# Seventeen loads of a recurrence-and-feed-forward kernel, issued by ScalarE in place of SyncE

## The chip, the core and the metric

One core of one Trainium2 chip. A core has five engines that run beside each other and meet through semaphores: TensorE (PE, matmuls), VectorE (DVE), ScalarE (ACT), GpSimd (POOL) and SyncE (SP, which here only issues transfers). Sixteen DMA engines move the data. A transfer is issued by an instruction of SP or of ACT, each of which has a queue of its own to the DMA engines. The metric is the device time of one execution in microseconds, median of the runs; less is better.

## The reference, cut to what matters

```python
# 4 batches, 8 heads, 768 positions, 48 channels
for t in range(S):
    state = alpha[:, :, t, :, None] * state + np.einsum('bhd,bhe->bhde', k[:, :, t], v[:, :, t])
    y[:, :, t] = np.einsum('bhd,bhde->bhe', q[:, :, t], state)
x = y.transpose(0, 2, 1, 3).reshape(3072, 384)
h = np.maximum(np.maximum(x @ w1, x @ w2), x @ w3)      # 384 -> 768
out = h @ w_out                                         # 768 -> 384
```

A gated linear recurrence over 768 positions, then a feed-forward layer that takes the maximum of three products. All tensors are float32.

## The kernel before, in words

The positions are cut into 6 blocks of 128. A *unit* is one block of one batch, with its 8 heads: 24 units, u = 0 to 23. Two neighbouring units make a *group*, n = 0 to 11, and are loaded together.

For each group four tensors are loaded: a (alpha), k, q and v, 128 positions by 16 heads by 48 channels, 384 KB each. A row of one head has 48 floats, so every piece that the DMA engines move has 192 bytes. Groups 0 to 3 are loaded in halves of 192 KB (one unit each; "load k 2 8" is the second half of k of group 2), groups 4 to 11 whole. There are four buffers of each tensor, so the load of group n waits until group n - 4 has been read. The weights (four matrices of 1.2 MB, in two pieces each) are loaded among the first two groups.

What is done with a unit, with the lines of the profile:

- ACT takes the logarithm of a (L398, "ln"); PE sums it along the positions (L438, "cums" and L408, "totals"); ACT takes exponentials (L443 "ep", L446 "en", L414 "e").
- DVE or POOL multiply q and k by them (L450); POOL or ACT scales v (L457, L460).
- PE turns the scaled q and k (L479), or a DMA transpose does ("cross", L469, issued by SP); ACT or DVE copies them (L486).
- PE makes the scores (L495), DVE masks them (L500), PE multiplies with v and adds what the state gives (L541, L538, "outs"); the state itself is carried by L600, L607 and L613.
- The result is copied (L552, L554), turned (L568, L573) and goes through the feed-forward layer: PE (L638, "grow"), ACT (L649) and DVE (L654), then PE (L674, "shrink"), a copy by ACT or DVE (L689) and the store (L694), 192 KB a unit.

The feed-forward layer uses w2 - w1 and w3 - w1, and w1 @ w_out folded into one matrix (L329, L337, L362, L368, L379, L386).

Every step is entered in a `Plan` with a list of engines that could do it. The table `ORDER` gives the order in which the steps are put into the program, and `PICK` the place in that list of the engine taken, where it is not the first. Each engine then runs its own instructions in that order and waits by semaphores. So a step's place in `ORDER` sets only its place among the instructions of its own engine. `load_options` lists who can issue a load: before, SP alone. Stores can be issued by ACT or SP. The transfers of SP and ACT share eight semaphores in turn, by their order in `ORDER`: a transfer waits until the one that stands eight before it has landed, whichever engine issued that.

SP issues its transfers strictly one after the other: an issue that waits holds back those behind it. The same holds for ACT, where an issue stands between computing steps.

Of the kernel before, what the change touches and what calls it, by code (L numbers as in the profile page):

```python
# [32 lines left out]


ORDER = (
# [44 lines left out]
)  # L80
BANKS = (
# [9 lines left out]
)  # L91
PICK = {
# [8 lines left out]
}  # L101

HARD, HARD_LOAD, HARD_LATE, LATE_FROM = 0.5, 1.8, 1.5, 3


def load_options(share, n):
    return [("SP", HARD, 0, HARD_LOAD * share, HARD_LATE * (n >= LATE_FROM))]  # L110


def weight_options(share, cast):
# [57 lines left out]
def kernel(  # L171
# [125 lines left out]
    def load(n):  # L297
        cb, g = divmod(n, B // UB)
        pieces = [(i * H, (i + 1) * H) for i in range(UB)] if n < HALF_LOADS else [(0, HG)]
        for lo, hi in pieces:  # L300
            for x in "akqv":
                t = ld[x][n % LOADED]
                plan.step(f"load {x} {n} {lo}", load_options((hi - lo) / HG, n), n,
                          lambda e, x=x, t=t, lo=lo, hi=hi: engines[e].dma_start(  # L304
                              t[:, lo:hi],
                              views[x][cb * P:(cb + 1) * P, g * HG + lo:g * HG + hi]),
                          writes=[(x, n % LOADED, h) for h in range(lo // H, hi // H)])
# [455 lines left out]
```

## Time and profile before

| | |
|---|---|
| time, median of 3 runs | 152.29 us (152.26 to 152.42) |
| span of the profiled execution | 466.5 us (its time beside the span is not given) |
| TensorE busy in it | 457.5 us, 1683 matmuls |
| VectorE, ScalarE, GpSimd busy | 112.5, 90.1, 48.0 us |
| loads and weights (queue of SP) | 27.27 MB in 113232 packets |
| stores and constants of ACT (queue of ACT) | 3.54 MB in 2880 packets |
| packets under 512 bytes | 109712 of 116131 |

The span runs from the first to the last instruction. In this profiled execution it is three times as long as a timed run. A row of the timeline gives start, length, engine, line, operation and tile; SPq and ACTq are the issues of transfers by SP and ACT, and the length of such a row is the time that the issuing engine spends on it, not the transfer. "Us to landing" is the time from the issue to the last byte.

### The profile page before, as it was taken

To read this page: it belongs to the slowest core of one execution; us is meant where nothing else is said; L and a number is where in the kernel's file an instruction comes from. 1 tells how busy PE (TensorE), PEld (TensorE's weight loads), DVE (VectorE), ACT (ScalarE), POOL (GpSimd) and SP (SyncE) were. 2 spreads that over 40 slices of the span, in tenths; PEclk is the share of its full clock that TensorE was granted. 3 is DMA by queue.
4 is the path that set the end of the run, shared out by engine and by line. 5 is a ranking of instruction groups with operands and counts; after the bars stand their busy time and mean duration, and the time that the engine had idled before them with its cause. 6 is when DMAs were issued, how large, how long until landed. Compare 5 with 4: busy or idle time off the path is not lost.

```text
span 466.5 us, 4171 instructions
## 1 busy us (share of the span) xinstructions
PE 457.5 (98%) x1683; PEld 263.5 (56%) x1683; DVE 112.5 (24%) x196; ACT 90.1 (19%) x177; POOL 48.0 (10%) x72
## 2 busy tenths in 40 slices
PE   4999999999999999999999999999999999999997
PEld 1667556674555656547546645545546554567473
DVE  5420313131123122222412221322221321231100
ACT  4323221122121312111212200121220111001010
POOL 0110002003001030210111120011110020000000
DMA  9999500540087000700032640020550030100001
GB/s 179 272 287 209 110 0 1 111 76 1 0 163 124 1 0 18 152 17 35 0 60 49 141 91 9 2 62 0 112 112 17 18 79 25 35 0 25 1 34 34
DMA packets 116131, 31.07 MB, mean 67 GB/s; under 512 B 109712, under 2 KB 114960, under 8 KB 116112
## 3 DMA queue, kind: packets, MB, share of 16 engines
q1 hardware_dynamic: 113232, 27.27, 27.9%
q10 hardware_dynamic: 2880, 3.54, 2.2%
q8 instruction: 13, 0.21, 0.2%
q14 instruction: 6, 0.05, 0.0%
HBM read 23.69 MB, written 4.72 MB: 61 GB/s over the span
## 4 chain that ended last, share of the span: by engine, by line
PE 98%; DMA 1%; SPq 0%; DVE 0%; issue 0%; DVEq 0%
PE psum L638 38%; PE psum L674 29%; PE psum L479 6%; PE psum L495 4%; PE psum L582 4%; PE psum L541 3%; PE psum L438 3%; PE psum L568 3%; PE psum L600 3%; PE psum L538 2%; PE psum L379 2%; DMA qn<-in_q_dram 1%; PE psum L362 1%; PE psum L408 1%; SPq L304 0%; DVE qk L450 0%
## 5 line engine op out<-in xcount | busy, mean ns | idle before, releaser
L638 PE MATMUL psum<-xT,wd 128*128 128x256 f16 (+1 forms) x540 | 186.4, 602 | 0.0
L638 PEld LDWEIGHTS <-wd 128*128 128x128 f16 x540 | 105.1, 209 | 67.5 <-issue 61.5
L674 PE MATMUL psum<-wo,hT 128*128 128x384 f16 (+1 forms) x150 | 96.7, 887 | 0.0
L674 PEld LDWEIGHTS <-hT 128*128 128x128 f16 x150 | 34.4, 230 | 54.6 <-issue 52.0
L674 PE MATMUL psum<-w1o,xT 128*128 128x384 f16 (+1 forms) x75 | 50.1, 847 | 0.0
L654 DVE TENSOR_TENSOR hT<-psum,hT 128x512 f16<-128x512 f32 (+1 forms) x39 | 24.7, 647 | 99.7 <-PE psum L638 99.7
L649 ACT ACTIVATE hT<-psum 128x512 f16<-128x512 f32 (+1 forms) x39 | 21.7, 564 | 111.0 <-PE psum L638 111.0
L500 DVE TENSOR_TENSOR LA<-psum,c 128x1024 f16<-128x1024 f32 x24 | 28.9, 1221 | 41.0 <-PE psum L495 28.7
L541 PE MATMUL psum<-v,LA 128*128 128x48 f16 x192 | 30.3, 314 | 0.0
L541 PEld LDWEIGHTS <-LA 128*128 128x128 f16 x192 | 26.5, 179 | 5.7 <-issue 5.1
L613 POOL TENSOR_TENSOR Z<-U,G 48x192 f16<-48x192 f32 x26 | 14.1, 543 | 109.5 <-DVE U L607 108.5
L438 PE MATMUL psum<-la,c 128*128 128x384 f16 x24 | 19.9, 847 | 4.3 <-ACT la L398 4.3
L479 PE MATMUL psum<-c,qk 128*128 128x128 f16 x96 | 22.1, 480 | 1.7 <-DVE qk L450 1.7
L479 PEld LDWEIGHTS <-qk 128*128 128x128 f16 x96 | 16.9, 208 | 9.1 <-DVE qk L450 4.0
L450 POOL TENSOR_TENSOR qk<-qn,ep 128x384 f16<-128x384 f32 x11 | 10.9, 994 | 105.2 <-ACT ep L443 94.0
L674 PEld LDWEIGHTS <-xT 128*128 128x128 f16 x75 | 13.1, 185 | 14.7 <-issue 14.2
L582 PE MATMUL psum<-Z 128*128 128x384 f16 x27 | 20.2, 869 | 0.0
L443 ACT ACTIVATE ep<-psum 128x384 f32<-128x384 f32 x24 | 11.7, 494 | 41.3 <-PE psum L438 41.2
L689 ACT COPY ob<-psum 128x384 f32<-128x384 f32 (+1 forms) x18 | 8.3, 469 | 54.7 <-PE psum L674 54.7
L554 DVE TENSOR_SCALAR xb<-psum,c 128x384 f16<-128x384 f32 x15 | 9.2, 617 | 37.9 <-PE psum L541 37.9
L568 PE MATMUL psum<-c,xb 128*128 128x128 f16 x63 | 17.5, 455 | 0.0
L446 ACT ACTIVATE en<-psum 128x384 f32<-128x384 f32 x24 | 11.5, 490 | 28.4 <-PE psum L438 27.1
(61 smaller groups left out, 297.2 us busy)
## 6 DMA issues: line engine op xcount, KB each, us to landing
out_dram<-ob ACTq DMA_DIRECT2D x17, 192.0 KB, 1.9
an<-in_alpha_dram SPq DMA_DIRECT2D x8, 384.0 KB, 5.3
kn<-in_k_dram SPq DMA_DIRECT2D x8, 384.0 KB, 5.4
qn<-in_q_dram SPq DMA_DIRECT2D x8, 384.0 KB, 5.7
vn<-in_v_dram SPq DMA_DIRECT2D x8, 384.0 KB, 4.2
ws<-in_moe_w_dram SPq DMA_DIRECT2D x3, 768.0 KB, 6.7
an<-in_alpha_dram SPq DMA_DIRECT2D x8, 192.0 KB, 4.0
kn<-in_k_dram SPq DMA_DIRECT2D x8, 192.0 KB, 4.0
```

What stands on the lines that cost most here:

```text
L438: nc.tensor.matmul(live[Lk], tri, la[:, hs, :D], start=True, stop=True)
L479: nc.tensor.transpose(live[tk][:, w, j, :], qk[:, w, 2 * j:2 * j + 2, :], ident)
L495: nc.tensor.matmul(live[Ak][:, p, j * P:(j + 1) * P], qkT[rows, 1, j, :], qkT[rows, 0, j, :], start=True, stop=True)
L500: lambda e: nc.vector.tensor_mul(LA.rearrange("p a b t -> p (a b) t"), live[Ak].rearrange("p a (b t) -> p (a b) t", t=P), maskA.unsqueeze( ...
L541: nc.tensor.matmul(yp[:, 2 * j + p, :], LA[:, p, j, :], v16[:, 2 * j + p, :], start=(cb == 0), stop=True, skip_group_check=True)
L568: nc.tensor.transpose(live[xk][:, ft, :], xb[:, ft * P:(ft + 1) * P], ident)
L582: nc.tensor.matmul(live["wm"], zero[:, :P], zero, start=True, stop=True)
L613: lambda e, rows=rows, cols=cols: engines[e].tensor_mul(Zn[rows, :, cols], (Us[u % 3] if cb else live[pk])[rows, :, cols], G[rows, i * NP: ...
L638: nc.tensor.matmul(live[gk][:, jj, :], wd[:, kt, g, j * P:(j + 1) * P], xT[:, kt, :], start=(kt == 0), stop=(kt == NFT - 1))
L649: lambda e, h=h, gk=gk: nc.scalar.activation(out=h, in_=live[gk], func=AFT.Relu),
L654: lambda e, h=h, gk=gk: nc.vector.tensor_max(h, live[gk], h),
L674: nc.tensor.matmul(live[ok][:, cols], a[:, i * P:(i + 1) * P], w[:, cols], start=(kt == 0), stop=(kt == nk - 1))
```

## The change

`load_options` gets ACT as a second choice, and `PICK` takes it for seventeen loads: six halves (of groups 2 and 3) and eleven whole ones (of groups 4 to 11). All of them stand behind the loads of the weights. About half of them stand where a packet of TensorE's instructions comes. `ORDER` places them, and some stores, anew among the steps of ACT.

```diff
 def load_options(share, n):
-    return [("SP", HARD, 0, HARD_LOAD * share, HARD_LATE * (n >= LATE_FROM))]
+    return [("SP", HARD, 0, HARD_LOAD * share, HARD_LATE * (n >= LATE_FROM)), ("ACT", 0.45, 0, HARD_LOAD * share)]
 PICK = {
...
+    19: 1, 21: 1, 25: 1, 27: 1, 28: 1, 30: 1, 235: 1, 300: 1, 365: 1, 367: 1,
+    486: 1, 488: 1, 544: 1, 545: 1, 547: 1, 604: 1, 662: 1,
...
 }
```

What this makes of the engines' programs: PE, DVE and POOL have the same instructions in the same order. ACT has its computing steps in the same order, with the seventeen loads between them; ten or so of its stores stand some steps earlier or later. SP has seventeen issues fewer. By their order the moved loads are: k 2 (second half), a 3 (second half), v 2 (first half), k 3 (first half), q 3 (second half), v 3 (first half), and then q 4, k 5, k 6, v 6, v 8, a 9, k 8, k 9, k 10, v 9 and k 11. A part of the order on ACT, where the first of them stand:

```diff
 L649 Activation hT
+L304 DMACopy kn<-in_k_dram 128x8x48
 L414 Activation e
 L398 Activation la<-an 128x8x48
...
 L446 Activation en
+L304 DMACopy an<-in_alpha_dram 128x8x48
 L414 Activation e
+L304 DMACopy vn<-in_v_dram 128x8x48
 L649 Activation hT
```

105 rows, old and new, of tables (ORDER, PICK) are left out of this document.

## The prediction

> **What bounds the kernel now.** I read the engine totals and the granted clock first, because the span and the times do not fit.
>
> ```profile
> span 466.5 us, 4171 instructions
> PE 457.5 (98%) x1683; PEld 263.5 (56%) x1683; DVE 112.5 (24%) x196; ACT 90.1 (19%) x177; POOL 48.0 (10%) x72
> core 0: 466.5 us, clock 1.000
> 68.74 0.63 PE psum L438
> ```
>
> The span is 466.5 us and the median of the runs is 152.29 us. The page gives no other time for the profiled execution. The clock column reads 1.000, yet TensorE (PE) is busy 457.5 us, which cannot fit into 152.29, so PE ran at least three times slower there than in the timed runs. The profile's shares are therefore not those of the timed run: a stage that PE bounds shrinks, what the DMA engines and the other engines need does not. So I work out differences and add them to the median.
>
> The second view is the DMA row and the stages by window.
>
> ```profile
> DMA  9999500540087000700032640020550030100001
> 0.00:34.00 34.00, 28.00 (x132) 16.31 (x133) 14.85 (x35) 12.23 (x20) 3.98 (x8) 1.00 0.99 247
> 34.00:53.00 19.00, 19.00 (x86) 13.53 (x82) 1.76 (x2) 5.79 (x10) 1.00 (x1) 1.00 1.04 206
> 160.00:350.00 190.00, 190.00 (x683) 105.61 (x682) 47.62 (x76) 37.35 (x74) 26.54 (x38) 1.00 0.25 53
> ```
>
> The columns are the length, then the busy time of PE, PEld, DVE, ACT and POOL, the clock, the DMA share and GB/s. Up to 53 us the 16 DMA engines are full (0.99 and 1.04). That stretch does not shrink with a faster PE: it is a floor under the start.
>
> How much faster PE is follows from the first load of group 2, a 2, and its reader.
>
> ```profile
> 27.49 3.81 SPq L304 DMA_DIRECT2D an<-in_alpha_dram  x2
> an<-in_alpha_dram SPq DMA_DIRECT2D x1, 192.0 KB, 6.5
> 68.42 0.95 PE L438 MATMUL psum<-la,c 128*128 128x384 f16 x1
> L398 ACT ACTIVATE la<-an 128x384 f16<-128x384 f32 x8 | 4.1, 524 | 2.2 <-DMA an<-in_alpha_dram 2.2
> ```
>
> a 2 lands at 27.49 + 6.5 = 34.0; its logarithm takes 0.52, so the matmul "cums 4" (at 68.42 in the profile) cannot start before 34.5 in a timed run. Behind it stand 466.5 - 68.4 = 398.1 us of the profile. They fit into 152.29 - 34.5 = 117.8 us, so r, the length of PE's work in a timed run over that in the profile, is at most 117.8 / 398.1 = 0.296. I take 0.25 to 0.296. The lower end is an estimate: at 0.25 the 398.1 take 99.5, and 18.3 us are left for PE's waits, the last stores and what lies outside the span, more than I can account for.
>
> The Trainium skill, "TensorE: Matmul & The Clock Gate", section "Seeing it yourself", reports the clock gate stuck at a quarter for 50 us and more. 384 columns in 0.63 us are 610 a microsecond, a quarter of that page's 2.4 GHz, so the trace agrees although the clock column shows nothing; by it r would be 0.25, an estimate.
>
> So a timed run has two parts: a start of about 34.5 us that the DMA engines set, and a rest of PE's order with waits. In 160 to 350, PE would need 190 x 0.25 to 0.296 = 47.5 to 56.2 us, DVE is busy 47.6 and ACT 37.4. DVE is near its limit and ACT has a fifth to a third free.
>
> **The change part by part.** By the order of the programs, PE, DVE and POOL are untouched, and ACT's computing steps keep their order. Seventeen loads (six half ones of 192 KB, eleven of 384 KB) leave SP's queue for ACT's; some stores of ACT stand elsewhere among its steps. Up to the second half of q 2, SP's order differs by nothing but the first moved load, k 2, which ACT issues ahead of a 2's logarithm while a 2 is still under way (at most 0.97 - 0.38 if it is not covered). The start up to 34.5 us stays: 0.
>
> *ACT's time for issuing.* Nothing in the trace shows a load on ACT; stores there and loads on SP are the nearest rows.
>
> ```profile
> 264.57 0.49 ACT L446 ACTIVATE en<-psum 128x384 f32<-128x384 f32 x1 [0.17 <-PE psum L438]
> 264.58 0.34 ACTq L694 DMA_DIRECT2D out_dram<-ob  x1
> 264.95 0.60 ACT L457 ACTIVATE v<-vn,c 128x384 f16<-128x384 f32 x1
> 0.74 0.46 SPq L304 DMA_DIRECT2D an<-in_alpha_dram  x1
> 7.26 0.97 SPq L304 DMA_DIRECT2D qn<-in_q_dram  x1
> 131.07 0.37 SPq L304 DMA_DIRECT2D vn<-in_v_dram  x1
> 131.54 1.29 SPq L304 DMA_DIRECT2D kn<-in_k_dram  x1
> 141.89 1.67 SPq L304 DMA_DIRECT2D kn<-in_k_dram  x1
> ```
>
> The store is issued beside the exponential before it: the next ACTIVATE starts 0.38 after that one, without a gap. So an issue of up to 0.38 is covered by the ACTIVATE ahead of it; if ACT stands idle there, it is free. A full load takes 0.37 into an empty queue, 1.29 right behind another, 1.67 in a long row; a half one 0.46 to 0.97. Lower bound: 0. Upper bound: 11 x (1.67 - 0.38) + 6 x (0.97 - 0.38) = 14.2 + 3.5 = 17.7 us of ACT's time. ACT's queue is mostly empty, so I take the row of the empty queue, except for four loads that stand a few steps behind another one (v 2 behind a 3, q 4 behind v 3, k 6 behind k 5, a 9 behind v 8): 4 x (1.29 - 0.38) = 3.6, and 0.05 for the other thirteen, together 4.3. Queued behind each on ACT are exponentials, relus and copies out of PSUM, for which PE and DVE wait. With a fifth to a third of ACT free, I put a fifth of it on the path: +0.9 us. Ends: 0, and a third of 17.7 = 5.9.
>
> *Loads that come later.* On SP a load runs ahead of the computing; on ACT it waits for its place among the steps. The tightest is the first half of v 2, behind "e 2", which needs "totals 2".
>
> ```profile
> 75.83 0.57 PE L408 MATMUL psum<-c,la 128*128 128x2 f16 x8
> 38.34 0.93 SPq L304 DMA_DIRECT2D vn<-in_v_dram  x1
> vn<-in_v_dram SPq DMA_DIRECT2D x1, 192.0 KB, 3.5
> DMA to landing us min/median/max: 3.0/5.0/7.5
> 100.79 0.37 PE L541 MATMUL psum<-v,LA 128*128 128x48 f16 x2
> L460 POOL TENSOR_SCALAR v<-vn,c 128x384 f16<-128x384 f32 x14 | 8.5, 613 | 4.3 <-DMA vn<-in_v_dram 3.9
> ```
>
> Totals 2 comes (75.83 + 0.57 - 68.42) x 0.25 to 0.296 = 2.0 to 2.4 after cums 4, at 36.5 to 36.9; with ACT's exponentials ahead of it the load goes out near 37.4 and lands by the median of 5.0 at 42.4, against 38.34 + 3.5 = 41.8 before. It is needed (100.79 - 68.42) x 0.25 to 0.296 = 8.1 to 9.6 after cums 4, less POOL's 0.61: at 42.0 to 43.5. Late by -1.1 to +0.4; I take +0.2, and for a landing after 7.5 up to 2.9.
>
> *Loads that come earlier.* What stays on SP moves up by what is taken out ahead of it. The tightest is a 6: before, four full loads after k 4.
>
> ```profile
> 47.78 1.59 SPq L304 DMA_DIRECT2D kn<-in_k_dram  x1
> 134.50 3.75 SPq L304 DMA_DIRECT2D an<-in_alpha_dram  x2
> 177.44 0.95 PE L438 MATMUL psum<-la,c 128*128 128x384 f16 x1
> L398 ACT ACTIVATE la<-an 128x768 f16<-128x768 f32 x8 | 6.8, 844 | 0.0
> ```
>
> k 4 lands about 47.78 + 5.0 = 52.8; four full loads at 3.75 / 2 = 1.87 each make a 6 land near 60.3, two stores between them some 0.4 each: 61.1. "cums 13" needs it at 34.5 + (177.44 - 68.42) x 0.25 to 0.296 = 61.8 to 66.8, less 0.84: 61.0 to 66.0. So it is hardly late before (0.1 at most, 4.9 early at best); I take -0.3 for this and the loads like it, bounds 0 and -1.9, one full load.
>
> The Trainium skill, "DMA: Bandwidth & Descriptors", section "Issuing engines are not separate DMA queues", says that issuing from several engines saves only sequencer time, as all share the same 16 DMA engines; by it this -0.3 would be 0 and the time 153.4, an estimate.
>
> *Stores moved on ACT.* Each still goes out beside a step (0.34, covered as above): 0; uncovered, the few of them cost 0.34 each.
>
> Sum: +0.9 + 0.2 - 0.3 = +0.8, so 152.29 + 0.8 = **153.1 us**.
>
> **The rivals.**
> *Faster: SP's single row was late.* If r is nearer 0.25 and several loads like a 6 wait now, each is brought forward by one full load. Place: cums 13 and the like; price: up to -1.9, with ACT's part small: 150.4 to 151.9, say 151.3. For it: full DMA engines in the start, a margin of nothing at r = 0.25. Against it: 18.3 us of waits at that r would move every need later, and the DMA engines stay as full.
> *Slower: ACT's queue fills.* If loads from two queues share full engines, each drains at half the rate, and the issue on ACT takes 1.29 to 1.67 as in SP's row. Then ACT loses up to 17.7 us in the middle of the kernel; it decides from about 0.8 us an issue. A quarter to a third of it on the path: +4 to +6, about 157. Against it: a load into an empty queue took 0.37.
> *Slower: a packet of PE's instructions comes late.*
>
> ```profile
> q8 instruction: 13, 0.21, 0.2%
> ```
>
> Thirteen packets took 0.2% of 16 x 466.5 us, about 1.1 us each, in a queue of their own beside SP's; with a third queue filled perhaps half as much again: if PE waited for each, +0.5 x 13 = 7, if for one or two +1. Against it: no wait in the profile names one.
> *Nothing happens*: the loads were never near the path and all issues are covered: 152.3.
>
> **How the numbers follow.** 0.2% is 0.3 us, about what a measurement of this kernel can tell from no change. Forecast (152.6 to 154.0, with 151.9 to 152.6 at its lower edge): 0.42, of which 0.32 slower, 0.07 the same, 0.03 faster. Faster rival: 0.28. ACT's queue fills: 0.14. Packets or a late load of 1 to 3 us: 0.08, slower. Nothing happens: 0.08, the same. That gives faster 0.31, same 0.15, slower 0.54. The range reaches from 151.0 (most of the faster rival) to 156.0 (part of the full queue); what is left out is the worst of both, about 2 in 10. The forecast's own range is 151.9 to 154.0.
>
> **What would show it.** Issues of loads on ACT of 0.37 to 0.6, the next ACTIVATE starting without a gap, show the cover right; 1.3 and more show the second rival. Load a 2 landing near 34 shows the start unchanged. If the profile is again one with a slow PE, waits of PE in it say little, and the time alone decides between the forecast and the faster rival. Wrong would be a time below 151.9 or above 154.0, above all PE waits on ACT's lines 443, 446 and 649 behind a load.

## The result and the profile after

| | |
|---|---|
| before, beside the change | 151.94 us, median of 20 runs |
| after | 152.58 us, median of 20 runs (151.58 to 153.63) |
| ratio | 1.0056, 95% interval 1.0035 to 1.0076 |

The change costs 0.56% by the ratio on record, or 0.85 us (the two medians alone lie 0.64 us apart); on the 152.29 us of the prediction that makes 153.1. Ratios are always to the kernel before on the same chip, since before took 151.9 us on two chips and 154.9 and 155.0 on two others. They leave out runs with a disturbed clock, and one kernel below had too few others for a ratio.

The page of the kernel after (engine totals, DMA row, the queues of SP and of ACT):

```profile
PE 134.1 (89%) x1683; PEld 104.3 (69%) x1683; DVE 108.7 (72%) x196; ACT 88.2 (58%) x177; POOL 49.1 (33%) x72
DMA  5999999999999999989999489999999999251032
q1 hardware_dynamic: 84288, 21.76, 70.5%
q10 hardware_dynamic: 31824, 9.05, 27.1%
```

This profiled execution took 152.63 us with a span of 150.8, so PE ran at its timed rate. PE is busy 89% of it, and the DMA engines are full, with few gaps, to the 34th of 40 slices, far beyond the 53 us that the profile of before with its slow PE had shown. 5.51 MB have moved from SP's queue to ACT's.

The stages behind the start, from the windows of after (length, then busy time of PE, PEld, DVE, ACT, POOL, clock, DMA share, GB/s):

```profile
40.00:50.00 10.00, 10.00 (x146) 8.07 (x145) 6.54 (x14) 7.09 (x15) 4.07 (x5) 1.00 1.16 213
62.00:74.00 12.00, 9.19 (x125) 7.33 (x121) 7.70 (x14) 6.40 (x14) 4.12 (x7) 1.00 1.10 222
74.00:90.00 16.00, 16.00 (x214) 13.01 (x214) 14.24 (x25) 9.58 (x19) 8.57 (x11) 1.00 1.03 199
90.00:130.00 40.00, 39.93 (x494) 31.53 (x492) 33.98 (x57) 23.98 (x52) 17.83 (x26) 1.00 1.14 213
```

PE idles in one place, 2.81 us between 62 and 74. What holds it there (waits of PE in after, 58 to 76 us: total, times, longest):

```profile
PE psum L567 <- ACT xb L551: 1.5, 1, 1.5
PE psum L599 <- ACT e L413: 0.8, 1, 0.8
PE psum L478 <- ACT e L413: 0.5, 1, 0.5
```

All three are waits for ACT. The timeline of ACT and its queue in after shows why (the bracket is the idle time before the step, and what ended it):

```profile
66.66 0.40 ACTq L693 DMA_DIRECT2D out_dram<-ob  x1
67.16 0.58 ACT L551 ACTIVATE xb<-psum,c 128x384 f16<-128x384 f32 x1 [2.40 <-DMA vn<-in_v_dram]
68.36 0.36 ACTq L693 DMA_DIRECT2D out_dram<-ob  x1
68.77 0.27 ACT L413 ACTIVATE e<-psum,c 128x16 f32<-128x16 f32 x1 [1.02 <-DMA qn<-in_q_dram]
70.96 0.41 ACTq L303 DMA_DIRECT2D vn<-in_v_dram  x1
71.42 0.61 ACT L456 ACTIVATE v<-vn,c 128x384 f16<-128x384 f32 x1 [1.51 <-DMA an<-in_alpha_dram]
71.76 4.34 ACTq L693 DMA_DIRECT2D out_dram<-ob  x1
76.15 0.60 ACT L648 ACTIVATE hT<-psum 128x512 f16<-128x512 f32 x1 [2.23 <-PE psum L637]
80.35 2.90 ACTq L693 DMA_DIRECT2D out_dram<-ob  x1
```

The bracket at "xb" names v 5, the one at "e" names q 6 and the one at "v" names a 7, but none of these steps reads them. What waited for the loads is the transfer ahead of each step: store 2 (66.66), store 5 (68.36) and load v 6 (70.96). Each goes out 0.02 us after a load of SP has landed, by SP's timeline, the transfers (size, us to landing) and the chain of waits of after:

```profile
56.76 3.40 SPq L303 DMA_DIRECT2D vn<-in_v_dram  x1
vn<-in_v_dram SPq DMA_DIRECT2D x1, 384.0 KB, 9.9
60.26 8.07 DMA qn<-in_q_dram
65.23 3.43 SPq L303 DMA_DIRECT2D an<-in_alpha_dram  x2
an<-in_alpha_dram SPq DMA_DIRECT2D x1, 384.0 KB, 5.7
```

v 5 lands at 56.76 + 9.9 = 66.7, q 6 at 68.33, a 7 at 65.23 + 5.7 = 70.9. These three loads stand eight transfers ahead of store 2, store 5 and load v 6 and have the same semaphores. The order that counts is that of the built program, not that of `ORDER`, in which v 5 is only four ahead of store 2:

```
v 5 (SP), k 5, q 6 (SP), a 7 (SP), k 6, a 8 (SP), q 7 (SP), k 7 (SP), store 2, q 8 (SP), store 5, v 6
```

In the kernel before, store 2 shared its semaphore with k 4 and store 3 with v 4, landed long ago. So ACT, standing at a transfer, loses 4.9 us here to loads that it doesn't need. My theory is that this makes the loss ("ACT waits for a semaphore whose load is still under way"). Four more loads on ACT go out 0.02 us after the transfer with their semaphore has landed (v 3, q 4, k 5 and a 9, at 45.09, 48.88, 54.96 and 79.64), but there PE has no gap. Two more rows look bad: the stores at 71.76 (0.8 us behind load v 6) and 80.35 (0.7 behind a 9) took 4.34 and 2.90 us to issue. Such a row begins while steps ahead of it still run: of the 4.34 us ACT worked until 73.93 and then stood 2.23, until 0.05 us after the issue had ended; the bracket at 76.15 puts it down to PE. The rivals: those held issues are the cost; q 6 and its neighbours land late, whoever waits; the new order costs, not the loads.

### The profile page after: what moved, and what is told of

It is laid out like the page before. It is cut to its first block, busy times and chain, and to the rows that moved or that the text cites. A ratio compares the mean times of both kernels' runs of the same rounds, so it can differ in the third digit from the quotient of the medians.

```text
span 150.8 us, 4164 instructions
## 1 busy us (share of the span) xinstructions
PE 134.1 (89%) x1683; PEld 104.3 (69%) x1683; DVE 108.7 (72%) x196; ACT 88.2 (58%) x177; POOL 49.1 (33%) x72
## 4 chain that ended last, share of the span: by engine, by line
PE 68%; DMA 12%; SPq 9%; DVE 3%; issue 2%; ACT 1%; POOL 1%; ACTq 1%; DVEq 0%
PE psum L637 27%; PE psum L673 21%; SPq L303 8%; DMA qn<-in_q_dram 5%; DMA an<-in_alpha_dram 4%; PE psum L494 3%; PE psum L478 3%; DMA xT<-xb 3%; PE psum L540 2%; PE psum L537 2%; PE psum L378 2%; PE psum L599 2%; PE psum L567 2%; PE psum L437 2%; SPq L322 1%
## 5 line engine op out<-in xcount | busy, mean ns | idle before, releaser
L637 PE MATMUL psum<-xT,wd 128*128 128x256 f16 (+1 forms) x540 | 54.5, 251 | 2.3 <-DVE wd L336 1.7
L637 PEld LDWEIGHTS <-wd 128*128 128x128 f16 x540 | 42.8, 98 | 8.1 <-DVE wd L336 2.1
L673 PE MATMUL psum<-wo,hT 128*128 128x384 f16 (+1 forms) x150 | 27.7, 320 | 0.0
L673 PEld LDWEIGHTS <-hT 128*128 128x128 f16 x150 | 14.5, 98 | 8.9
L673 PE MATMUL psum<-w1o,xT 128*128 128x384 f16 (+1 forms) x75 | 15.8, 319 | 0.0
L397 ACT ACTIVATE la<-an 128x384 f16<-128x384 f32 (+1 forms) x16 | 10.9, 688 | 4.7 <-DMA an<-in_alpha_dram 4.6
L437 PE MATMUL psum<-la,c 128*128 128x384 f16 x24 | 8.1, 346 | 4.2 <-ACT la L397 4.2
L478 PE MATMUL psum<-c,qk 128*128 128x128 f16 x96 | 8.8, 241 | 3.2 <-DVE qk L449 2.7
L540 PE MATMUL psum<-v,LA 128*128 128x48 f16 x192 | 11.2, 183 | 0.0
L551 ACT ACTIVATE xb<-psum,c 128x384 f16<-128x384 f32 x9 | 5.2, 582 | 9.2 <-PE psum L540 6.3
L540 PEld LDWEIGHTS <-LA 128*128 128x128 f16 x192 | 9.7, 96 | 0.8
```

Of the source, the lines that this page charges most:

```text
L478: nc.tensor.transpose(live[tk][:, w, j, :], qk[:, w, 2 * j:2 * j + 2, :], ident)
L540: nc.tensor.matmul(yp[:, 2 * j + p, :], LA[:, p, j, :], v16[:, 2 * j + p, :], start=(cb == 0), stop=True, skip_group_check=True)
L637: nc.tensor.matmul(live[gk][:, jj, :], wd[:, kt, g, j * P:(j + 1) * P], xT[:, kt, :], start=(kt == 0), stop=(kt == NFT - 1))
L673: nc.tensor.matmul(live[ok][:, cols], a[:, i * P:(i + 1) * P], w[:, cols], start=(kt == 0), stop=(kt == nk - 1))
```

## The experiments

**The kernel before at PE's timed rate.** Unchanged.

> The kernel before, unchanged, for a profile at TensorE's full rate (span near 150 us). My theory (ACT's issues and later loads cost): every store is issued on ACT in 0.34 to 0.4 us, none in over 1 us, and the 16 DMA engines are as full as after (share 0.9 and more up to about 125 us). The rival that ACT's queue fills behind a load: the same, no long store on ACT. The rival that the order of the loads decides: q 6 lands before about 68.3 us, where it lands after the change.

Measured 155.17 us, span 153.4, on a chip where before takes 152.3 to 158.2 us, with a median of 154.86. The same four stages, and the chain of waits at v 2:

```profile
40.00:50.00 10.00, 8.75 (x125) 6.61 (x124) 7.26 (x15) 7.21 (x15) 2.32 (x3) 1.00 0.87 170
62.00:74.00 12.00, 12.00 (x180) 10.12 (x178) 10.23 (x19) 8.81 (x18) 6.75 (x10) 1.00 1.08 224
74.00:90.00 16.00, 15.57 (x199) 12.58 (x197) 13.53 (x24) 9.86 (x20) 7.79 (x11) 1.00 0.98 206
90.00:130.00 40.00, 38.24 (x469) 30.09 (x468) 32.98 (x54) 22.40 (x48) 17.53 (x26) 1.00 1.09 211
38.25 6.36 DMA vn<-in_v_dram
```

Here PE has no gap between 62 and 74, but idles 1.25 us behind v 2 (issued 38.25, landed 44.6), and 0.43 and 1.76 us later (the 1.76 at two transposes that SP issues). No store on ACT takes over 0.46 us to issue. And q 6 lands only at 67.00 + 7.0 = 74.0 us here, later than the 68.33 after the change, without a gap of PE: that speaks against a late q 6 as the cause. So the change closes about 3.4 us of gaps and opens 2.8, which would make it faster and not slower. This is one execution on a slower chip; how much of the 3.4 before has where it takes 151.9 us, no trace shows.

**All loads back on SP, the new order kept.**

```diff
 PICK = {
...
-    19: 1, 21: 1, 25: 1, 27: 1, 28: 1, 30: 1, 235: 1, 300: 1, 365: 1, 367: 1,
-    486: 1, 488: 1, 544: 1, 545: 1, 547: 1, 604: 1, 662: 1,
...
```

> The changed kernel with all seventeen loads given back to SP, the order of the steps and the stores as changed. If the issuing on ACT costs the 0.56% (my theory, and also the rival of the full queue): 0.998 to 1.001 of before. If the moved stores and the new order of the loads cost it: still 1.004 to 1.007.

Measured 1.0048 (0.9996 to 1.0100). The new order without its loads is no better than before, and by its time it can't be told from the whole change. Its trace tells the two apart: PE is busy 12.00 of the 12 us from 62 to 74, and idles 1.04 us between 40 and 50 and 1.39 between 90 and 130 instead.

**Stores ahead of the whole loads.** In the order of the steps on ACT:

```diff
+store 3
 load v 6
...
-store 3
+store 4
 relu 8 0
 load v 8
...
-store 4
```

> The changed kernel with two stores put ahead of a load on ACT instead of behind one: store 3 right ahead of load v 6, store 4 ahead of load v 8. After the change these two were issued in 4.34 and 2.90 us, in which ACT did nothing else. If these 7.2 us are the cost (the full queue): both stores at about 0.4 us, and 0.999 to 1.002 of before. If the cost lies in the other issues and in late loads: 1.004 to 1.007.

Measured 1.0022 (0.9982 to 1.0062), between the two forecasts. (That ACT "did nothing else" in those 7.2 us is misread: five ACTIVATEs ran during the first store's issue.) The 4.34 and 2.90 became 0.35 and 2.55, but ACT still waited 2.1, 1.1 and 1.7 us for v 5, q 6 and a 7, and PE was busy only 10.24 of the 12 us from 62 to 74:

```profile
62.00:74.00 12.00, 10.24 (x134) 8.39 (x132) 7.52 (x13) 6.49 (x15) 5.04 (x8) 0.88 1.12 220
```

So the held stores are not what opens that gap.

**The six halves alone.** The eleven whole loads back on SP.

```diff
 PICK = {
...
-    235: 1, 300: 1, 365: 1, 367: 1, 486: 1, 488: 1, 544: 1, 545: 1, 547: 1, 604: 1, 662: 1,
...
```

> Only the six half loads (groups 2 and 3) stay on ACT, the eleven whole ones are back on SP. If later first loads (v 2, v 3) cost: 1.003 and more, as most of the change. If whole loads on ACT cost, by the full queue or by their order: 0.998 to 1.002.

Measured 0.9977 (0.9934 to 1.0020) on that chip, and on another:

> Only the six halves on ACT, all eleven whole loads on SP, beside the run with six halves and eight whole ones. If the halves alone bring what the best run gains: 0.990 to 0.996 of the kernel before, within 0.003 of that run. If the eight whole loads bring a part of their own, by clearing SP's row: 0.996 to 1.000.

0.9909 (0.9863 to 0.9955). So the halves alone gain, up to about 1%; on the first chip the interval still includes no change at all.

**The changed kernel again**, beside the next three.

> The changed kernel once more, on the chip of the runs beside it, as their yardstick. Both theories: ratio to the kernel before 1.003 to 1.008, and in the trace three waits of ACT for loads that SP has issued, 2.4, 1.0 and 1.5 us, between 64 and 72 us, with two waits of PE for ACT of 1.5 and 0.8 us just behind them.

Measured 1.0038 (1.0000 to 1.0075). ACT again waited 2.8, 1.0 and 1.4 us for v 5, q 6 and a 7 at the same three transfers, and PE behind the first two of them 1.87 and 0.51.

**The eleven whole loads alone.** The six halves back on SP.

```diff
 PICK = {
...
-    19: 1, 21: 1, 25: 1, 27: 1, 28: 1, 30: 1,
...
```

> Only the eleven whole loads on ACT, the six halves back on SP. Here the semaphores that store 2, store 5 and load v 6 on ACT get were last used by k 5, a 6 and k 6, which have landed by then, not by v 5, q 6 and a 7. Theory 'ACT waits for a semaphore whose load is still under way': no wait of ACT over 0.7 us for a load between 60 and 75 us, so the eleven whole loads cost little: 0.998 to 1.004 of the kernel before. Rival 'issuing whole loads on ACT costs, wherever they wait': without the gain of the halves the whole ones show their full cost, 1.010 to 1.015.

No ratio (151.5 to 156.3 us over six runs; the trace is of one of 154.14), so its time decides nothing between the two forecasts. The waits for v 5 and q 6 are gone and PE is busy 12.00 of 12 us from 62 to 74. But the expectation missed that store 3 now has the semaphore of a 7, and load v 8 that of a 8 (timelines of ACT and PE, windows of this run):

```profile
75.61 0.34 ACTq L693 DMA_DIRECT2D out_dram<-ob  x1
76.00 0.60 ACT L648 ACTIVATE hT<-psum 128x512 f16<-128x512 f32 x1 [2.34 <-DMA an<-in_alpha_dram]
78.24 0.40 ACTq L303 DMA_DIRECT2D vn<-in_v_dram  x1
78.74 0.48 ACT L688 COPY ob<-psum 128x384 f32<-128x384 f32 x1 [2.14 <-DVE xb L553]
79.27 0.82 PE L637 MATMUL psum<-xT,wd 128*128 128x256 f16 x6 [1.13 <-ACT ob L688]
74.00:90.00 16.00, 14.56 (x195) 11.41 (x190) 13.24 (x22) 9.04 (x18) 8.36 (x11) 1.00 1.08 210
```

ACT stands 2.34 us at store 3 and 2.14 at load v 8, which goes out 0.02 us after a 8 (issued 68.49) has landed, and PE waits 1.13 us for the copy behind it. It is the same kind of wait, at two other transfers, with the gap of PE moved behind the second. PE also idles 1.69 us between 50 and 62 here, 1.40 of it behind the first half of v 3, which is back in SP's row.

**Three transfers a few steps later.** All seventeen loads stay on ACT; the other engines' programs are unchanged.

```diff
 xb 9
-store 2
 xb 8
-store 5
 e 5
 relu 6 0
 ep 12
-load v 6
 v 10
 e 6
 relu 8 1
+store 2
+store 5
 relu 8 2
+load v 6
 en 12
 en 13
 store 3
```

> The changed kernel with three transfers of ACT a few steps later: stores 2 and 5 behind relu 8 1, load v 6 behind relu 8 2; the seventeen loads stay on ACT and PE, DVE, POOL and SP keep their programs. By then the loads whose semaphores they share (k 5, q 6, a 7) have landed. Theory 'ACT waits for a semaphore whose load is still under way': the three waits of 4.9 us of ACT and PE's waits of 1.5, 0.8 and 0.5 us behind them go, the kernel gains 1.5 to 2.8 us on the changed one: 0.987 to 0.996 of the kernel before. Rival 'q 6 and its neighbours land late, whoever waits' (DMA engines full): PE then waits elsewhere for them, the ratio stays at 1.003 to 1.008.

Measured 0.9986 (0.9950 to 1.0022), 0.5% below the changed kernel on that chip (0.9986 / 1.0038; the two intervals just overlap). Windows and ACT's timeline of this run:

```profile
62.00:74.00 12.00, 12.00 (x170) 9.81 (x168) 9.79 (x18) 8.03 (x18) 5.84 (x9) 1.00 1.10 210
74.00:90.00 16.00, 15.14 (x195) 12.13 (x194) 14.10 (x24) 10.01 (x21) 7.33 (x10) 1.00 1.13 220
72.33 0.40 ACTq L303 DMA_DIRECT2D vn<-in_v_dram  x1
72.89 3.12 ACTq L693 DMA_DIRECT2D out_dram<-ob  x1
76.05 0.60 ACT L648 ACTIVATE hT<-psum 128x512 f16<-128x512 f32 x1 [2.40 <-PE psum L637]
```

With the same loads landing at much the same times (q 6 at 69.0), the 2.81 us gap is gone. That speaks for the waits and against the rival that the loads land late, whoever waits. The gain is smaller than expected, and 0.86 us of a gap opens behind 74: store 3, 0.56 us behind v 6, takes 3.12 us to issue, relu 8 0 stands behind it (ACT idles 2.40 us), PE waits 0.5 and 0.3 us for ACT, and now ACT is not late anyway. Load v 6 still goes out 0.02 us after a 7 has landed.

**Three loads back on SP.** k 5, k 6 and v 6; six halves and eight whole loads stay on ACT.

```diff
 PICK = {
...
-    300: 1, 365: 1, 367: 1,
...
```

> The changed kernel with k 5, k 6 and v 6 back on SP, fourteen loads left on ACT. Stores 2, 5 and 3 now share semaphores with a 6, k 5 and q 6, which have landed by then, and no store stands right behind v 6 any more. Theory 'ACT waits for a semaphore whose load is still under way': no wait of ACT over 0.7 us for a load between 60 and 75 us, 0.987 to 0.997 of the kernel before. Rival 'late loads': k 5 and k 6 in SP's row push q 6 to 70 us, PE waits for them, 1.003 to 1.010.

Measured 0.9916 (0.9885 to 0.9946), and on a second chip:

> The kernel with k 5, k 6 and v 6 back on SP once more (six halves and eight whole loads on ACT), on the chip of the three runs beside it, as their yardstick: 0.989 to 0.995 of the kernel before, and no wait of PE over 0.4 us behind 46 us.

0.9794 (0.9736 to 0.9853). This version beats both kernels, by more than expected on the second chip. It has the new order too, so the order does not cost wherever the loads are. Its windows, and ACT's queue in the stage in question, on the second chip:

```profile
40.00:50.00 10.00, 9.74 (x131) 7.32 (x130) 7.13 (x15) 7.45 (x16) 2.89 (x5) 1.00 1.16 226
62.00:74.00 12.00, 12.00 (x171) 9.96 (x169) 10.77 (x18) 8.47 (x19) 7.11 (x10) 1.00 1.00 221
74.00:90.00 16.00, 16.00 (x207) 13.16 (x205) 14.26 (x26) 10.71 (x22) 8.03 (x12) 1.00 1.27 229
90.00:130.00 40.00, 40.00 (x490) 31.14 (x487) 33.88 (x57) 22.71 (x49) 16.83 (x26) 1.00 1.07 210
65.91 0.36 ACTq L693 DMA_DIRECT2D out_dram<-ob  x1
67.10 0.36 ACTq L693 DMA_DIRECT2D out_dram<-ob  x1
70.92 0.34 ACTq L693 DMA_DIRECT2D out_dram<-ob  x1
```

Stores 2, 5 and 3 go out without a wait, and PE has no gap from 50 to 130 us. Load v 8 still waits for a 8, whose semaphore it has (ACT stands 0.73 us there), and a store still takes 2.93 us to issue (at 78.78, behind a 9), both without cost here.

**The eight whole loads alone.** As the version above, with the halves on SP too.

> Only the eight whole loads q 4, v 8, a 9, k 8, k 9, k 10, v 9 and k 11 on ACT, all halves back on SP. If the halves bring the gain: 1.000 to 1.006 of the kernel before, as with all loads on SP in this order (1.0048). If the eight whole ones bring it: 0.990 to 0.996.

Measured 1.0155 (1.0093 to 1.0217), slower than either forecast, so the halves belong to the gain. PE waits 2.87 us for POOL behind the second half of q 3:

```profile
57.21 0.61 PE L477 MATMUL psum<-c,qk 128*128 128x128 f16 x4 [2.87 <-POOL qk L448]
```

SP issued it at 48.38, and it landed 7.64 us later, at 56.0, while q 4, issued on ACT 0.7 us behind it, landed at 55.9. Behind this gap PE's granted clock is a half for some 5 us (last section), and in all six runs the mean clock is 0.976 to 0.989, so a part of the 1.55% may be that lower clock. The halves alone gave 0.9909 there and both together 0.9794: the eight whole loads help beside the halves, and without them they cost.

**Store 3 ahead of v 6**, on top of the three transfers a few steps later.

```diff
 relu 8 2
-load v 6
+store 3
 en 12
+load v 6
 en 13
-store 3
```

> All seventeen loads on ACT. As in the run with three transfers a few steps later, but store 3 stands ahead of load v 6 instead of right behind it. Theory 'a store right behind a whole load in ACT's queue holds ACT': the issue of store 3 takes 0.3 to 0.6 us instead of 3.1, relu 8 0 no longer waits 2.4 us, PE's waits of 0.5 and 1.2 us at 76 us go, 0.990 to 0.996 of the kernel before. Rival 'the issue is held because all 16 DMA engines are full, whatever stands ahead': the issue of store 3 still takes 2 to 4 us and the ratio stays at 0.996 to 1.002. In between, if load v 8, now 3 us behind v 6, is held instead.

Measured 0.9869 (0.9806 to 0.9931), 0.8% behind the version with three loads back, on one chip and with overlapping intervals. Windows and timeline of ACT:

```profile
62.00:74.00 12.00, 11.94 (x168) 9.66 (x166) 9.40 (x18) 8.17 (x19) 5.50 (x9) 1.00 1.03 210
74.00:90.00 16.00, 14.54 (x186) 11.44 (x184) 13.68 (x22) 8.93 (x19) 7.91 (x10) 1.00 1.17 220
72.43 0.34 ACTq L693 DMA_DIRECT2D out_dram<-ob  x1
72.84 0.42 ACTq L303 DMA_DIRECT2D vn<-in_v_dram  x1
74.47 2.22 ACTq L303 DMA_DIRECT2D vn<-in_v_dram  x1
76.79 0.48 ACT L688 COPY ob<-psum 128x384 f32<-128x384 f32 x1 [2.46 <-DVE Z L612]
```

The in-between outcome: the issue of store 3 fell from 3.12 to 0.34 us at the same time of the kernel, so the load ahead of it in ACT's queue held it, not the full DMA engines. Load v 8, 1.6 us behind v 6, takes 2.22 us to issue instead, and PE loses 1.46 us there. (Store 3 and load v 8 also each go out 0.02 us after the load with their semaphore, a 7 and a 8, has landed.)

## Why the prediction was right, and where it was not

The sign and the size came out; the sum was right for other reasons than its terms, so the hit is in good part luck. Nor do the gaps of the two traces, 3.4 us closed and 2.8 opened, add up to the measured +0.85: that balance is not shown.

- *PE's rate, the stage behind the start.* Right. 1683 matmuls take 134.1 us where the slow profile had 457.5: 0.293, inside 0.25 to 0.296. The chain of waits of after has a cums of 384 columns back to back at 0.16 us, against 0.63 then: 0.25, as the Trainium skill's stuck clock ("TensorE: Matmul & The Clock Gate", "Seeing it yourself") would have it.
- *The start, 0.* Right within what runs differ by: cums 4 starts at 33.49 in after and 34.64 in the kernel before at full rate, forecast not before 34.5; in the other traces at full rate it starts between 33.75 and 36.01.
- *ACT's issuing, +0.9.* The mechanism held for the loads and the term was mis-sized: v 2, q 4, k 6 and a 9, which I priced at 1.29, took 0.61, 0.38, 0.37 and 0.40, and all others but one (0.83) 0.37 to 0.43. What I priced at 0 to 0.34, a store behind a load, took 4.34 and 2.90. In after that is hidden; with ACT on time it costs PE 0.9 us (three transfers later).
- *Later loads, +0.2.* Not borne out. In after v 2 is issued on ACT at 36.09 and lands 5.6 us later at 41.7, and PE has no gap between 40 and 50 us; in the one trace of before at full rate it landed at 44.6. Over all traces the sign is open: with v 2 on ACT it landed between 41.6 and 43.9 us (nine traces), with v 2 on SP between 41.9 and 44.6 (four). My 41.8 for before came from the profile with a slow PE, where v 2 landed 3.5 us after its issue, against 6.4 at full rate. Why is open: from 38 to 45 us the DMA engines were no less busy there (share 1.05, 208 GB/s) than at full rate (0.84, 164 GB/s).
- *Earlier loads, -0.3.* a 6 lands 53.13 + 6.8 = 59.9 instead of 58.97 + 5.4 = 64.4, yet before has no gap of PE from 62 to 74: no gain at this place. The gaps that close between the two traces lie at v 2 and behind 74 us. The Trainium skill ("DMA: Bandwidth & Descriptors", "Issuing engines are not separate DMA queues") says that issuing from several engines saves only the issuing sequencer's time; the missing gain at a 6 agrees, but the version with three loads back, 0.8 and 2.1% faster than before, shows that here more than nothing was to be had.
- *Stores moved, 0.* This is the step that failed, and with it the assumption that a load on ACT "waits for its place among the steps" and for nothing else. I had described the shared semaphores and did not work out which load each store, or load v 6, would wait for. It is the largest term: 4.9 us of ACT and 2.81 us of PE, and taking it away (three transfers later, three loads back) gained 0.5% and 1.2% on the changed kernel (the second also takes whole loads off ACT's queue, so not all of it is these waits).
- *The rivals.* "ACT's queue fills" happened at two stores, not in every issue; it did not make the kernel lose the 4 to 6 us of that rival. The packets of PE's instructions (13, 0.6% of the engines' time) show in no wait of PE. "SP's single row was late" was half right: by the one trace of before at full rate up to 3.4 us were to be had, and the new waits cost 2.8.
- *What would show it wrong.* PE waits on ACT's lines behind a load were named; they came, but at L551 and L413 (the forecast named 443, 446 and 649), and mostly behind stores that waited for loads of SP.

Open are: the part of the gain that before leaves on a chip where it takes 151.9 us; why before differs by 3 us between chips while the version with three loads back took 150.5 and 151.0; and the split between halves and whole loads.

## What to carry to other kernels

Before a transfer goes to a computing engine's queue, or stores there move, write down for every transfer on that engine which earlier one shares its semaphore, in the order of the built program, and when that lands: the engine's steps wait for it, needed or not. Keep transfers on such an engine some 2.5 us apart behind a large load, as far as this kernel shows. Put there the loads that a long row on SP would make late (here the halves), and leave on SP those whose place makes a store wait.

## What the runs showed of the hardware

How long the issue of a transfer on ACT takes goes with how closely it follows a whole load (384 KB, 2048 pieces of 192 bytes) in ACT's own queue. From the nine runs with at least eight whole loads on ACT, 47 to 125 us:

| distance behind the latest whole load on ACT | issue of the transfer |
|---|---|
| 0.56 to 1.77 us, 10 cases | 1.85 to 4.34 us |
| 1.92 to 2.23 us, 10 cases | 0.36 to 2.00 us |
| 2.51 to 5 us, 46 cases | 0.36 to 0.46 us |

SP had 0.6 to 1.2 MB in flight in the first row, 0.8 to 1.0 in the second and 0.2 to 1.3 in the third, so it is not SP's load alone. Nor does a long issue on SP hold one on ACT: in after, k 6 took 0.37 us at 58.30, in the midst of v 5's 3.40 us on SP. Three kinds of case don't fit. A store 0.4 us behind another store took 1.36 us once. Behind 125 us, stores 19, 18 and 16 follow closely on each other, and the second or third of them takes 1.00 to 1.84 us in eleven of the twelve traces of the new order. And with the halves on SP in the new order, store 1 near 42 us takes 2.3 to 3.2 us although nothing of ACT is shortly ahead of it. In the run with all loads on SP:

```profile
43.57 3.17 ACTq L692 DMA_DIRECT2D out_dram<-ob  x1
```

Loads of the two queues share the engines and don't land in the order of their issue: k 6, issued on ACT at 58.30, landed at 65.4, ahead of v 5, issued by SP at 56.76 and landed at 66.7. The Trainium skill ("DMA: Bandwidth & Descriptors", "Queues, rings and completion order") says that each DMA engine goes round between the queues that have work, which agrees.

A gap of PE can cost more than its length. The windows behind three gaps, in the eight whole loads alone, in the changed kernel again and in after (the granted clock is the third number from the end):

```profile
57.00:62.00 5.00, 4.45 (x31) 3.27 (x32) 1.26 (x2) 2.07 (x3) 1.69 (x3) 0.50 1.03 223
70.00:74.00 4.00, 3.75 (x34) 3.10 (x34) 2.49 (x6) 2.33 (x6) 0.00 (x0) 0.57 1.22 292
70.00:74.00 4.00, 3.17 (x30) 2.10 (x29) 2.75 (x6) 2.51 (x6) 0.05 (x1) 1.00 1.25 274
```

In the first PE had waited 2.87 us, in the second 1.87 and 0.51, and the granted clock fell to about a half. In after the waits were 1.48 and 0.51 us, and 0.83 within the window, and it stayed at 1.00. The second execution took 154.22 us, against a median of 152.76 for that kernel. These are single traces; what decides whether the clock falls is not shown.
